# Mask copies by ScalarE into PSUM and a new written order for the first phase of a fused attention and feed-forward kernel

## The chip, the core and the metric

The kernel runs on one core of one Trainium2 chip. The core has a matrix engine (TensorE, in the profile PE, with its weight loads as PEld), VectorE (DVE), ScalarE (ACT), GpSimd (POOL), SyncE (SP, which only starts transfers here), and 16 DMA engines that all queues share. The engines work through their own instruction streams in order and wait for one another on semaphores. Matmul results land in PSUM, which has eight banks of 128x512 float32 here; everything else lies in SBUF.

The metric is device time in microseconds, the median of several runs. Less is better.

## The reference

Two computations follow each other. First a banded attention: 8 batches, 8 heads, 576 positions, head size 64, float32; a query sees itself and the 63 positions before it. Then a feed-forward layer on the 4608 rows of 512 that come out:

```python
scores = scale * np.matmul(q, k.transpose(0, 1, 3, 2))
mask = (rel >= 0) & (rel < window)            # rel = query - key, window = 64
scores = np.where(mask, scores, -1000000000.0)
scores = scores - np.max(scores, axis=-1, keepdims=True)
attn = np.exp(scores)
attn = attn / (np.sum(attn, axis=-1, keepdims=True) + 1e-09)
attn_out = np.matmul(attn, v)
...
h = x @ w_in                                  # 4608x512 @ 512x2048
g = np.maximum(0.01 * h, h)
out = g @ w_out                               # 4608x2048 @ 2048x512
```

`w_in` and `w_out` come as float64 and are turned into float32 on the chip.

## The kernel before, in words

**Attention.** The work is cut into 72 units, one unit being 64 queries of one batch against the 128 keys that its band can touch, all eight heads at once. Two units make a pair `m`; a pair's scores fill two tiles, one for the even and one for the odd heads, numbered `b = 2m` and `b = 2m + 1`. Scores lie with the keys on the partitions, so the maximum over keys goes across partitions, which GpSimd does.

**Feed-forward.** Each float32 factor is split into a high and a low part, and a product is three matmuls. The rows are taken in nine chunks of 512. The first three are computed plainly (`mm1` for the first layer, `mm2` for the second), a later part of the kernel does the others with fewer products. Weights are made ready in 32 pieces, each in seven steps: `raw` (transfer from HBM), `bits`, `sign` (VectorE), `abs` (ScalarE), `clamp`, `join` (VectorE), `chi` (high part, ScalarE, and for even pieces a transfer of the joined weights to HBM), `rest` (low part, VectorE). Both operands of all these VectorE steps lie in SBUF.

**The order.** Two things set what stands where in the instruction streams. The first phase, in which pairs 0 to 7 go through attention and most weights are made ready, is written out by hand as the string `ORDER` (line 54); each word is a step and a number, and each engine, and each DMA queue, gets its steps in the order of the words. What stands behind the `|` of that string and all later work is put in order by a small planner (`arrange`) with its own estimates of durations; the change leaves that part alone. The words:

- `q`, `k`, `v`: loads for a pair, on SP. `raw` 0 to 2 also on SP, later ones on ScalarE's queue.
- `S` scores of a pair on PE, with the masks before them (`scores`, `add_mask`; lines 278 and 312 in the profile); `Z` adds the mask of pair 0 behind its scores; `X` idle matmuls on a zeroed tile that keep PE busy (line 503).
- `E` (`shield`, lines 322 and 324) takes a score tile from PSUM to SBUF, by VectorE for the first two, by ScalarE later; `P` the maximum over partitions on GpSimd (line 332); up to `b = 3` the maximum is subtracted by a matmul into the score bank (`N`, line 346), later by VectorE (`sub`, line 337); `exp` on ScalarE.
- `V` product with the values and the sums of a row (line 367, 16 matmuls a tile); `sm`, `rec`, `y` sum, reciprocal and division on VectorE, from PSUM; `T` turns the result (line 393); `H` and `L` split it into high and low part (ScalarE, VectorE; lines 397 and 401).
- `M` and `W` first and second layer of one piece (lines 431 and 467), `lk`, `gh`, `gl` the leaky step and its split in between (ScalarE, ScalarE, VectorE). The first six jobs are half chunks. `ev` takes a finished bank out.

**Masks.** The mask of a pair is added to its scores in PSUM: a matmul of the identity (`unit`) with the mask (`away`) opens the bank, and the 64 small matmuls of the scores accumulate on it. The tile of the even heads is the bank with tag `s`, that of the odd heads `t`; pairs 1 and 3 use two output banks (`o0`, `o1`). `turn` puts pairs 0 and 1 into the bank `o3` and all others into `s`.

**Loads.** Of the transfers on SP and ScalarE's queue, eight can be under way at a time; a ninth is issued when an earlier one has landed. A load of a tile that is used again also waits for the last matmuls that read it.

Of the kernel before, what the change touches and what calls it, by code (L numbers as in the profile page):

```python
# [59 lines left out]
sm6 sign5 sm7 rest4 rec7 rec6 rest3 M2 E8 abs5 y7 y6 T3 bits6 sign6 W1 lk2 H3 L3 clamp5 P8 M3 gh2 gl2 join5 v4 k5 q5  # L60
E9 S5 v5 q6 k6 raw8 lk3 gh3 chi5 abs6 sub8 bits7 exp8 gl3 M4 lk4 rest5 sign7 clamp6 W2 V8 P9 abs7 sub9 join6 gh4 raw9
M5 bits8 gl4 E10 sm8 sign8 exp9 chi6 W3 P10 clamp7 rec8 y8 join7 rest6 lk5 abs8 clamp8 gh5 V9 M6 W4 gl5 join8 bits9
sub10 sm9 sign9 rec9 y9 raw10 E11 raw11 chi7 P11 chi8 lk6 exp10 T4 gh6 abs9 rest8 rest7 bits10 M7 V10 W5 gl6 sign10
clamp9 H4 abs10 sub11 join9 L4 bits11 sm10 rec10 clamp10 y10 join10 lk7 raw12 exp11 gh7 gl7 S6 V11 chi9 rest9 sign11
W6 chi10 raw13 abs11 E13 E12 P12 rest10 sm11 bits12 clamp11 join11 rec11 y11 chi11 raw14 sign12 abs12 bits13 sign13
clamp12 sub12 join12 M8 T5 v6 q7 v7 k7 W7 lk8 gh8 H5 exp12 abs13 chi12 raw15 gl8 P13 bits14 L5 V12 sign14 clamp13
rest11 sub13 sm12 join13 rest12 rec12 S7 y12 E14 raw16 abs14 exp13 clamp14 join14 bits15 P14 W8 V13 M9 sub14 sm13
sign15 chi14 E15 exp14 chi13 abs15 lk9 gh9 P15 rec13 y13 V14 T6 rest14 rest13 sub15 M10 sm14 clamp15 gl9 rec14 join15
y14 exp15 raw17 H6 chi15 V15 W9 bits16 sign16 L6 lk10 gh10 abs16 raw18 sm15 rec15 gl10 y15 T7 H7 rest15 W10 clamp16
bits17 join16 sign17 L7 abs17 clamp17 join17 bits18 raw19 chi16 ev0 chi17 ev1 raw20 rest16 sign18 abs18 rest17 M11  # L70
bits19 clamp18 M12 lk11 gh11 gl11 lk12 gh12 sign19 join18 M13 W11 M14 gl12 abs19 raw21 chi18 lk13 bits20 clamp19
join19 chi19 raw22 sign20 rest18 rest19 W12 M15 gh13 gl13 abs20 W13 bits21 clamp20 sign21 join20 bits22 abs21 lk14
sign22 clamp21 join21 raw23 chi20 M16 gh14 gl14 W14 rest20 raw24 abs22 clamp22 join22 chi21 raw25 bits23 rest21 sign23
bits24 lk15 chi22 gh15 gl15 sign24 abs23 abs24 clamp23 join23 bits25 chi23 raw26 lk16 M17 W15 clamp24 sign25 rest22
# [30 lines left out]
def band_attention_ffn(ctx: ExitStack, tc: tile.TileContext, qk, vW, vL, w_in, w_out, eye_mask, out, outT):  # L105
# [162 lines left out]
    def quarter_scores(m, ps, begun, more=False):  # L268

        q = q_of(m)  # L270
        for w in range(UNITS):
            k = key_blocks(UNITS * m + w)
            for p in range(NP):
                for i in range(2):
                    for j in range(2):
# [2 lines left out]
                        nc.tensor.matmul(  # L278
                            ps[j][t, c : c + QB], k[i][s, p], q[s, w, p],
                            start=not begun and (not more or (w, p) == (0, 0)),  # L280
                            stop=not begun and not more or (w, p) == (UNITS - 1, NP - 1),
                        )
# [1144 lines left out]
```

## Time and profile before

| | |
|---|---|
| median of 3 runs | 850.51 us (849.96 to 850.99) |
| profiled execution | 850.4 us |
| its span, first to last instruction | 848.6 us |
| PE busy | 841.8 us, 99% |
| VectorE busy | 620.1 us, 73% |
| ScalarE busy | 375.7 us, 44% |
| GpSimd busy | 383.3 us, 45% |
| HBM read, written | 172.52 MB, 53.06 MB |

Times in the profile are microseconds from the start of the span. A line number names a line of the kernel before; `s<-away,unit` means that tile `s` is written from `away` and `unit`. Busy times of PE are modelled at their ends, so successive matmuls overlap; start to start is the time that a step takes on PE. Idle time of an engine is put down to what ended it.

The first phase lies in the first 130 us; the matmuls of the second chunk begin at 87.69 us.

### The profile page before, as it was taken

The page shows a single profiled execution, that of the slowest core. Times are in us where ns is not written, and L with a number is a line of the kernel's source. Part 1 is how long each engine was busy: PE and PEld are TensorE (multiplying, and loading weights), DVE is VectorE, ACT ScalarE, POOL GpSimd, SP SyncE. Part 2 cuts the span into 40 slices and gives each one's busy share as a digit, 9 for nine tenths or more (in the row PEclk, how much of TensorE's full clock was granted, in tenths as well). Part 3 has the DMA queues.
Part 4 walks back from the last instruction along what each step waited for, and adds up shares of the span by engine and source line. Part 5 has one row for each costly group of instructions (what it writes and reads, how often), then busy time and mean ns, then how long its engine had stood idle before and what let it go on. Part 6 is the DMA issues. An engine that isn't in the chain of part 4 may idle for free.

```text
span 848.6 us, 16788 instructions
## 1 busy us (share of the span) xinstructions
PE 841.8 (99%) x6778; PEld 686.3 (81%) x6778; DVE 620.1 (73%) x883; ACT 375.7 (44%) x605; POOL 383.3 (45%) x218
## 2 busy tenths in 40 slices
PE   8999999999999999999999999999999999999998
PEld 5887888888878888888888888888888888888886
DVE  6999885748768779867649987585679955446863
ACT  4665654333433354454444433443354533324431
POOL 5422000878888715587587757857111111111110
PEclk9999999999999999999999999999999999999999
DMA  9875756798899869999999999999998986777682
GB/s 324 273 233 155 253 162 235 264 284 271 288 307 323 301 212 286 314 305 317 333 351 358 365 351 318 365 310 311 242 272 235 238 248 196 198 198 198 193 211 92
DMA packets 127757, 226.80 MB, mean 267 GB/s; under 512 B 15552, under 2 KB 46400, under 8 KB 127680
## 3 DMA queue, kind: packets, MB, share of 16 engines
q0 software_dynamic: 51552, 90.18, 38.4%
q10 hardware_dynamic: 35664, 77.31, 27.9%
q1 hardware_dynamic: 40464, 58.24, 21.1%
q8 instruction: 53, 0.87, 0.4%
q14 instruction: 24, 0.20, 0.1%
HBM read 172.52 MB, written 53.06 MB: 266 GB/s over the span
## 4 chain that ended last, share of the span: by engine, by line
PE 97%; DVE 2%; DMA 0%; ACT 0%; issue 0%; ACTq 0%
PE m L1118 27%; PE z L1181 18%; PE acc L929 11%; PE h L920 11%; PE y L1138 10%; PE h L431 5%; PE acc L467 5%; PE s L278 4%; PE o L740 4%; PE o L367 1%; DMA qk<-qk 0%; PE t L393 0%; DVE raw L225 0%; PE s L312 0%; DVE w L242 0%; DVE raw L229 0%
## 5 line engine op out<-in xcount | busy, mean ns | idle before, releaser
L1118 PE MATMUL m<-pfew,p 128*128 128x512 f32 x720 | 169.4, 391 | 0.0
L1118 PEld LDWEIGHTS m<-pfew,p 128*128 128x128 f32 x720 | 134.5, 188 | 28.3
L1102 POOL DMA_DIRECT2D p<-w_first x42 | 31.8, 757 | 113.4 <-PE m L1118 61.0
L929 PE MATMUL acc<-p,gs 128*128 128x512 f32 x324 | 80.6, 394 | 0.0
L1127 DVE TENSOR_TENSOR p<-m,pxa 128x512 f32<-128x512 f32 x60 | 41.3, 689 | 47.0 <-PE m L1118 46.0
L681 POOL PARTITION_ALL_REDUCE g<-late_f x20 | 36.8, 1875 | 78.7 <-DVE late_f L666 72.0
L684 POOL PARTITION_ALL_REDUCE late_o<-late_f x20 | 66.1, 3329 | 12.2 <-ACT late_f L692 7.0
L1118 PE MATMUL m<-pxb,p 128*128 128x512 f32 x288 | 70.9, 391 | 0.0
L1130 ACT ACTIVATE p<-p 128x512 f32<-128x512 f32 x60 | 37.9, 631 | 73.6 <-DVE p L1127 73.5
L929 PEld LDWEIGHTS acc<-p,gs 128*128 128x128 f32 x324 | 59.8, 188 | 12.8
L1127 DVE TENSOR_TENSOR pxa<-m,pxa 128x512 f32<-128x512 f32 x60 | 41.4, 690 | 35.4 <-PE m L1118 34.7
L684 POOL PARTITION_ALL_REDUCE late_o<-e x18 | 59.5, 3336 | 8.5 <-ACT e L692 3.6
L1118 PEld LDWEIGHTS m<-pxb,p 128*128 128x128 f32 x288 | 53.7, 188 | 11.3
L684 POOL PARTITION_ALL_REDUCE late_o<-late_e x18 | 59.3, 3322 | 5.5 <-ACT late_e L692 5.2
L1181 PE MATMUL z<-gs,p 128*128 128x512 f32 x240 | 57.6, 389 | 0.0
L920 PE MATMUL h<-pxa,p 128*128 128x512 f32 x228 | 54.9, 390 | 0.0
L1102 POOL DMA_DIRECT2D p<-w_second x28 | 22.7, 811 | 68.5 <-PE z L1181 31.0
L1181 PEld LDWEIGHTS z<-gs,p 128*128 128x128 f32 x240 | 45.0, 188 | 9.4
L1181 PE MATMUL z<-third,p 128*128 128x512 f32 x216 | 51.9, 389 | 0.0
L1181 PE MATMUL z<-pxa,p 128*128 128x512 f32 x216 | 51.9, 389 | 0.0
L920 PEld LDWEIGHTS h<-pxa,p 128*128 128x128 f32 x228 | 42.7, 188 | 9.0
L1102 POOL DMA_DIRECT2D p<-w_sums x16 | 12.0, 747 | 80.2 <-PE z L1181 55.8
(193 smaller groups left out, 1775.3 us busy)
## 6 DMA issues: line engine op xcount, KB each, us to landing
p<-w_first POOLq DMA_DIRECT2D x42, 1024.0 KB, 6.9
p<-w_second POOLq DMA_DIRECT2D x28, 1024.0 KB, 8.3
p<-w_sums POOLq DMA_DIRECT2D x16, 1024.0 KB, 5.7
qk<-qk ACTq DMA_DIRECT2D x26, 512.0 KB, 5.8
pspare<-w_second ACTq DMA_DIRECT2D x16, 512.0 KB, 7.2
w_sums<-pspare ACTq DMA_DIRECT2D x16, 512.0 KB, 7.7
raw<-w_out ACTq DMA_DIRECT2D x15, 512.0 KB, 3.9
raw<-w_in ACTq DMA_DIRECT2D x14, 512.0 KB, 3.9
```

What stands on the lines that cost most here:

```text
L431: nc.tensor.matmul(ps, a[:, k, :], b[:, k, part], start=n == 0, stop=n == len(terms) - 1)
L467: nc.tensor.matmul(acc[c, i], a[:, ts], b, start=begin and n == 0, stop=end and n == 2)
L681: nc.gpsimd.partition_all_reduce(most_of(j), e_of(m)[:, j], P, ReduceOp.max)
L684: nc.gpsimd.partition_all_reduce(sum_of(j), e_of(m)[:, j], P, ReduceOp.add)
L920: nc.tensor.matmul(ps, a[:, k, :], b[:, k], start=i == 0, stop=i == len(terms) - 1)
L929: nc.tensor.matmul(acc[c, i], a[:, i * P : (i + 1) * P], b, start=begin and k == 0, stop=n in ends and k == 2)
L1102: nc.gpsimd.dma_start(to, of, max_dma_last_dim=2048)
L1118: nc.tensor.matmul(tiles[b], w[:, 256 * i + 128 * kt : 256 * i + 128 * kt + 128], x_part(OF_X[k], j, kt), start=begin and c == 0, stop=c = ...
L1127: nc.vector.tensor_tensor(to(), tiles[b], x(), ALU.add)
L1130: nc.scalar.activation(to(), to() if b is None else tiles[b], AF.Prelu, alpha=0.01)
L1138: nc.tensor.matmul(tiles[i], a, b, start=f == 0 and k == 0, stop=f == FT - 1 and k == 2)
L1181: nc.tensor.matmul(tiles[b + i], a, x, start=begin and f == 0 and c == 0, stop=f == half - 1 and c == 2, skip_group_check=not begin,)
```

## The change

Three edits and a new string.

1. `seed` (new, word `A`): for pairs 4 to 7 ScalarE copies the mask, repeated over the heads, from SBUF into the PSUM bank, and the scores accumulate on that. For pairs 4 and 5 it does so for both tiles, for pairs 6 and 7 for the odd heads' alone; the even heads' mask stays a matmul there.
2. `turn` of pairs 2 and 3 goes to the bank `o3` too, instead of `s`.
3. `ORDER` is new up to the `|`. It has the same words and four more, `A4` to `A7`. In each engine's stream steps change places: the first idle matmuls are nine ahead of `S0` and none behind it; four others move ahead of `V2`; `S1` comes ahead of `Z0`; `T2` and `V6` stand between `M0` and `M1`; VectorE's steps on weights and on attention are interleaved in another way; and SP's loads begin `q0 raw0 q1 k1 raw1 k3 raw2 k2 v1 v0 q2 k4 q3 v2` where they began `q0 k1 raw0 q1 raw1 v0 q2 k2 raw2 v1 k3 q3 v2`.

```diff
+SEEDED, TURNED_OVER = 4, 6
...
 ORDER = """
-q0 X6 S0 k1 raw0 q1 E0 P0 E1 bits0 sign0 raw1 v0 q2 k2 P1 X3 Z0 Z1 S1 abs0 E2 N0 exp0 X1 N1 bits1 sign1 abs1 clamp0
-join0 clamp1 V0 sm0 join1 exp1 V1 E3 S2 chi0 raw2 chi1 raw3 rec0 sm1 rec1 bits2 sign2 y1 y0 P2 P3 N2 raw4 E4 rest1
-rest0 E5 exp2 N3 exp3 T0 v1 V2 V3 k3 q3 abs2 H0 S3 v2 v3 q4 k4 sm2 P4 sub4 P5 rec2 sm3 L0 y2 rec3 clamp2 y3 exp4 V4 E6
-T1 join2 H1 sub5 sm4 bits3 rec4 L1 exp5 X4 V5 P6 raw5 chi2 sign3 abs3 E7 bits4 rest2 sub6 sm5 clamp3 rec5 y4 y5 sign4
-P7 M0 lk0 exp6 gh0 M1 abs4 gl0 T2 W0 join3 sub7 bits5 clamp4 V6 lk1 H2 exp7 raw6 L2 gh1 join4 V7 S4 chi4 raw7 chi3 gl1
...
+q0 X3 X6 raw0 S0 q1 k1 E0 P0 bits0 E1 sign0 P1 raw1 S1 Z0 abs0 k3 bits1 sign1 Z1 clamp0 raw2 k2 v1 N0 v0 E2 bits2 abs1
+sign2 P2 N1 join0 X1 exp0 V0 clamp1 exp1 V1 sm0 q2 E3 chi0 rec0 abs2 join1 S2 chi1 raw3 P3 y0 E4 P4 sm1 rest0 k4 q3
+clamp2 rec1 N2 N3 y1 exp2 rest1 v2 X4 raw4 exp3 E5 V2 q4 join2 V3 v3 T0 sm2 rec2 H0 sub4 S3 sm3 y2 rec3 exp4 L0 y3 V4
+k5 P5 A4 bits3 sub5 bits4 sm4 T1 E6 rec4 y4 H1 S4 exp5 P6 raw5 sign3 L1 V5 sub6 E7 chi2 sign4 exp6 abs3 sm5 rec5 P7 y5
+M0 rest2 T2 lk0 abs4 V6 gh0 clamp3 join3 clamp4 sub7 raw6 join4 chi3 gl0 exp7 chi4 bits5 M1 sign5 V7 sm7 rec7 rest4 y7
+E8 P8 q6 W0 lk1 sm6 H2 raw7 gh1 rec6 L2 y6 gl1 rest3 E9 M2 bits6 T3 abs5 lk2 H3 gh2 sign6 L3 q5 clamp5 join5 abs6
+clamp6 W1 A5 v4 gl2 sub8 join6 chi5 P9 M3 raw8 bits7 S5 lk3 exp8 sign7 raw9 gh3 chi6 rest5 gl3 abs7 M4 lk4 sub9 V8 sm8
...
     def scores(m):
-        if m in (1, 3):
-            ps = [ps_o.tile([P, 512], F32, tag=f"o{j}", name=f"s{m}_{j}") for j in range(2)]
-        else:
-            ps = [bank(t, f"s{m}_{j}") for j, t in enumerate("st")]
-        for j in range(2):
-            probs[2 * m + j] = ps[j]
+        open_scores(m, range(2 if m < SEEDED else m >= TURNED_OVER))
         if m == 0:
-            quarter_scores(m, ps, False, True)
+            quarter_scores(m, [probs[j] for j in range(2)], False, True)
             return
-        for x in ps:
-            add_mask(m, x, True)
-        quarter_scores(m, ps, True)
+        for j in range(2 if m < SEEDED else m >= TURNED_OVER):
+            add_mask(m, probs[2 * m + j], True)
+        seeded = () if m < SEEDED else range(m >= TURNED_OVER, 2)
+        quarter_scores(m, [probs[2 * m + j] for j in range(2)], True, skip=seeded)
+
+    def open_scores(m, which):
+        for j in which:
+            pool, tag = (ps_o, f"o{j}") if m in (1, 3) else (ps_e, "st"[j])
+            probs[2 * m + j] = pool.tile([P, 512], F32, tag=tag, name=f"s{m}_{j}")
+
+    def seed(m):
+        open_scores(m, range(m >= TURNED_OVER, 2))
+        a = mask_of(UNITS * m).bitcast(F32)
+        n = a.shape[1]
+        a = flat(a)[:, None, :].broadcast_to([P, H // n, n * QB])
+        for j in range(m >= TURNED_OVER, 2):
+            nc.scalar.copy(probs[2 * m + j].rearrange("a (b c) -> a b c", c=n * QB), a)
...
     def turn(m):
         y = ys.pop(m)
-        pool, tag = (ps_o, "o3") if m < 2 else (ps_e, "s")
+        pool, tag = (ps_o, "o3") if m < 4 else (ps_e, "s")
```

More of the change, by code (lines that the diff above doesn't have):

```diff
@@ L60 @@
[L60 to L74, printed above, removed]
@@ new lines @@
+k5 P5 A4 bits3 sub5 bits4 sm4 T1 E6 rec4 y4 H1 S4 exp5 P6 raw5 sign3 L1 V5 sub6 E7 chi2 sign4 exp6 abs3 sm5 rec5 P7 y5
+M0 rest2 T2 lk0 abs4 V6 gh0 clamp3 join3 clamp4 sub7 raw6 join4 chi3 gl0 exp7 chi4 bits5 M1 sign5 V7 sm7 rec7 rest4 y7
+E8 P8 q6 W0 lk1 sm6 H2 raw7 gh1 rec6 L2 y6 gl1 rest3 E9 M2 bits6 T3 abs5 lk2 H3 gh2 sign6 L3 q5 clamp5 join5 abs6
+clamp6 W1 A5 v4 gl2 sub8 join6 chi5 P9 M3 raw8 bits7 S5 lk3 exp8 sign7 raw9 gh3 chi6 rest5 gl3 abs7 M4 lk4 sub9 V8 sm8
+clamp7 E10 rec8 rest6 W2 y8 join7 bits8 M5 P10 gh4 exp9 chi7 gl4 V9 sign8 W3 lk5 M6 raw10 sm9 bits9 abs8 v5 E11 rec9
@@ new lines @@
+sub10 clamp8 gh5 join8 gl5 sign9 rest7 chi8 W4 exp10 abs9 y9 raw11 lk6 gh6 A6 v6 clamp9 join9 P11 bits10 sign10 V10
+raw12 rest8 W5 sub11 T4 abs10 k6 clamp10 H4 M7 join10 chi9 L4 sm10 q7 raw13 rest9 rec10 bits11 chi10 gl6 y10 exp11 lk7
+gh7 sign11 S6 V11 bits12 sign12 rest10 W6 abs11 clamp11 sm11 abs12 E12 rec11 M8 join11 y11 gl7 T5 E13 clamp12 W7 raw14
+bits13 A7 chi11 lk8 rest11 H5 sign13 abs13 join12 P12 sub12 L5 raw15 clamp13 k7 exp12 V12 gh8 bits14 S7 v7 gl8 q8 P13
+W8 join13 sign14 chi12 sub13 rest12 sm12 raw16 E14 abs14 chi13 rec12 y12 exp13 V13 clamp14 join14 P14 bits15 sm13
@@ new lines @@
+sign15 sub14 M9 chi14 raw17 E15 exp14 rest14 rec13 y13 abs15 bits16 lk9 clamp15 V14 rest13 T6 gh9 H6 P15 sm14 join15
+raw18 rec14 sub15 exp15 y14 chi15 gl9 M10 sign16 V15 abs16 L6 lk10 W9 sm15 rest15 bits17 rec15 y15 gh10 clamp16 gl10
+join16 T7 H7 L7 sign17 bits18 W10 raw19 sign18 ev0 chi16 abs18 abs17 M11 clamp17 lk11 join17 M12 bits19 ev1 raw20 gh11
+rest16 clamp18 M13 join18 gl11 W11 raw21 sign19 lk12 chi17 abs19 clamp19 rest17 gh12 gl12 join19 chi18 M14 bits21
+raw22 bits20 chi19 W12 lk13 sign20 gh13 sign21 gl13 rest19 abs20 abs21 clamp21 lk14 clamp20 rest18 join20 bits22 raw23
@@ L78 @@
+M16 sign22 chi20 join21 chi21 gh14 M15 gl14 rest20 abs22 clamp22 join22 raw24 W13 rest21 raw25 bits23 sign23 W14 abs23
+lk15 gh15 chi22 clamp23 gl15 bits24 sign24 W15 join23 lk16 abs24 M17 bits25 sign25 raw26 chi23 gh16 abs25 rest22
+clamp24 join24 gl16 clamp25 raw27 chi24 M18 lk17 rest23 bits26 join25 sign26 gh17 gl17 raw28 bits27 chi25 W16 abs26
+rest24 W17 v8 sign27 rest25 abs27 clamp26 lk18 gh18 clamp27 join26 join27 chi26 bits28 gl18 sign28 q9 chi27 rest26 k8
 |
@@ L262, in x_of, with quarter_scores @@
         return [x[:, :, w * QB : (w + UNITS) * QB] for x in xs[c]]
-    def quarter_scores(m, ps, begun, more=False):
+    def quarter_scores(m, ps, begun, more=False, skip=()):
         q = q_of(m)
@@ L280, in quarter_scores @@
                             start=not begun and (not more or (w, p) == (0, 0)),
-                            stop=not begun and not more or (w, p) == (UNITS - 1, NP - 1),
+                            stop=not begun and not more or (w, p) == (UNITS - 1, NP - 1), skip_group_check=j in skip,
                         )
@@ L508, in band_attention_ffn @@
     acts = dict(
-        S=scores, E=shield, Z=lambda b: add_mask(0, banks[b], False), P=top, N=take, sub=minus, exp=exps, V=values_q, sm=total, rec=inverse, y=product, T=turn, H=high_x, L=low_x,
+        A=seed, S=scores, E=shield, Z=lambda b: add_mask(0, banks[b], False), P=top, N=take, sub=minus, exp=exps, V=values_q, sm=total, rec=inverse, y=product, T=turn, H=high_x, L=low_x,
         raw=fetch_w, bits=bits, sign=sign, abs=size, clamp=clamp, join=join, chi=split, rest=rest, q=load_q, k=load_k, v=load_v,
```

3 lines of the change are left out of this document (removed).

## The prediction

> **What bounds the kernel now.** The page comes first: its span, and the chain of waits followed back from the last instruction. Then come the list of what the matmul engine (PE) waited for over the whole run, and the busy time of the engines in two stretches, 20.00 to 87.69 and 87.69 to 130 us. The columns of these two rows are PE, weight loads, VectorE (DVE), ScalarE (ACT), GpSimd (POOL), clock, DMA share and GB/s.
>
> ```profile
> span 848.6 us, 16788 instructions
> ...
> PE 97%; DVE 2%; DMA 0%; ACT 0%; issue 0%; ACTq 0%
> ```
>
> ```profile
> PE idle L503 <- DVE p L514: 1.5, 1, 1.5
> ...
> PE o L367 <- DVE sm L379: 0.2, 1, 0.2
> ```
>
> ```profile
> 20.00:87.69 67.69, 66.67 (x781) 53.86 (x781) 65.47 (x148) 44.17 (x82) 22.29 (x11) 1.00 0.69 212
> 87.69:130.00 42.31, 42.31 (x188) 35.07 (x187) 34.79 (x65) 23.22 (x39) 0.00 (x0) 1.00 0.70 228
> ```
>
> PE carries 97% of the chain, and its five waits (first and last row above), 2.9 us together, all lie ahead of 27 us. After that it is never idle, so whatever the first phase gains or loses goes through to the end one for one. Up to 87.69 us VectorE is busy for 65.47 of 67.69 us, so it is nearly as tight as PE: 2.2 us idle. After 87.69 it has 7.5 us free in 42. The change is therefore worth what it does to the start of the matmuls at 87.69 (M11 of the order).
>
> Four views of the first 34 us decide that. First the PE timeline (start, duration, line, operands, number).
>
> ```profile
> 1.45 2.93 PE L503 MATMUL idle<-p 128*128 128x512 f32 x6 [1.45 <-DVE p L514]
> 4.74 1.98 PE L278 MATMUL s<-qk 64*64 64x64 f32 x64 [0.37 <-DMA qk<-qk]
> ...
> 12.63 1.44 PE L367 MATMUL o<-v,e 128*64 128x65 f32 x32
> ...
> 15.76 1.13 PE L346 MATMUL s<-p,p 128*128 128x512 f32 x2
> ...
> 17.61 0.66 PE L393 MATMUL t<-unit,y 128*128 128x128 f32 x4
> 18.20 1.15 PE L367 MATMUL o<-p,p 128*64 128x65 f32 x32
> 19.28 0.73 PE L312 MATMUL s<-away,unit 128*128 128x512 f32 x2
> ...
> 22.36 1.17 PE L503 MATMUL idle<-p 128*128 128x512 f32 x4
> ...
> 26.60 1.69 PE L431 MATMUL h<-pxa,pfew 128*128 128x256 f32 x12 [0.47 <-ACT g L436]
> 28.13 0.60 PE L393 MATMUL t<-unit,y 128*128 128x128 f32 x4
> 28.49 1.63 PE L467 MATMUL acc<-pfew,gs 128*128 128x512 f32 x6
> 30.05 1.33 PE L367 MATMUL o<-p,e 128*64 128x65 f32 x32
> 31.30 0.73 PE L312 MATMUL s<-away,unit 128*128 128x512 f32 x2
> 31.96 0.27 PE L278 MATMUL s<-qk,p 64*64 64x64 f32 x2
> ...
> 33.05 1.96 PE L431 MATMUL h<-pxa,pfew 128*128 128x256 f32 x12
> ```
>
> Start to start, a pair of masks is 0.66 us (31.30 to 31.96), scores are 1.09 (to 33.05), a pair of values products (32 matmuls, V2 V3) 1.08 (18.20 to 19.28), so one V 0.55 to 0.6, two maxima subtractions (N2 N3) 1.85 (15.76 to 17.61), half a first layer (M1) 1.53 (26.60 to 28.13), half a second layer (W0) 1.56 (28.49 to 30.05), a turning (T2) 0.36.
>
> **The change part by part.** *The masks.* Pairs 4 and 5 lose two mask matmuls each, pairs 6 and 7 one each. Pair 4's are 0.66 us (above). The rows of pairs 5 and 6, each with the first row of the scores behind it:
>
> ```profile
> 38.50 0.63 PE L312 MATMUL s<-away,unit 128*128 128x512 f32 x2
> 39.06 0.27 PE L278 MATMUL s<-qk,qk 64*64 64x64 f32 x2
> ...
> 57.03 0.62 PE L312 MATMUL s<-away,unit 128*128 128x512 f32 x2
> 57.58 0.27 PE L278 MATMUL s<-qk,qk 64*64 64x64 f32 x2
> ```
>
> Pair 5 gives 0.56, pair 6 half of 0.55; for pair 7 I take pair 6's half to pair 4's, 0.28 to 0.33. That is 0.56 + 0.28 + 0.3 = 1.15 us for the pairs behind 33 us, and with pair 4 1.8 us. In their place ScalarE makes six copies of 128x512 into PSUM. No such copy from SBUF is in the trace; the nearest row writes PSUM from PSUM:
>
> ```profile
> 131.41 0.58 ACT L934 ACTIVATE h<-h 128x512 f32<-128x512 f32 x1 [3.99 <-PE h L920]
> ```
>
> Six at 0.5 to 0.6 are 3.0 to 3.6 us on an engine that is busy 44.17 of 67.69 us. Three of the four groups wait on nothing late. The first (A4) stands ahead of the shields of pair 3 and holds these, and so GpSimd's sixth and seventh maximum, by up to 1.1 us; I take 0.3, because the scores the shields read are done at about the same time. It can gain nothing there.
>
> *The loads.* The order also rearranges the SP queue, and this is the part I hold to be dearest. Before, its first loads are q0 k1 raw0 q1 raw1 v0 q2 k2 raw2 v1 k3 q3; after, q0 raw0 q1 k1 raw1 k3 raw2 k2 v1 v0 q2 k4 q3. The values of pair 0 (v0) go from sixth to tenth. The rows are the issues of raw1, v0 and v1 on SP, each with the time from issue to landing  (asked for one by one), and the engines' busy time from 10 to 12 us:
>
> ```profile
> 2.59 0.61 SPq L210 DMA_DIRECT2D raw<-w_out  x1
> DMA to landing us min/median/max: 6.9/6.9/6.9
> 3.25 0.67 SPq L174 DMA_DIRECT2D v<-vW  x1
> DMA to landing us min/median/max: 7.6/7.6/7.6
> 6.51 0.56 SPq L174 DMA_DIRECT2D p<-vW  x1
> DMA to landing us min/median/max: 9.0/9.0/9.0
> 10.00:12.00 2.00, 1.88 (x16) 0.82 (x9) 1.97 (x3) 1.55 (x4) 2.00 (x2) 1.00 1.05 403
> ```
>
> So raw1 lands at 9.5, v0 at 10.9, v1 at 15.5, with the DMA engines full (share 1.05). They land in the order of issue and are paced by bytes. In the changed queue the same 2272 KB stand up to raw1, and between raw1 and the landing of v0 lie k3, raw2, k2, v1 and v0 itself, 2064 KB. That is exactly what lies between raw1 and v1 before (v0, q2, k2, raw2, v1), which took 6.0 us. By the pace of v0 alone (520 KB in 1.36 us) it would be 5.4. So v0 lands between 14.9 and 15.5; I take 15.1. The first product with values (V0), at 12.63 before, waits for it, and all of PE stands behind it.
>
> [...]
>
> *The other moves at the front.* Nine idle matmuls instead of six stand ahead of the first scores. At 2.93 us for six they end by 5.8 at the latest; with the last one's end overlapped I take 5.4, so these scores start 0.7 us later than 4.74, and so does the whole chain of maxima (N1 near 13.3). The late v0 covers this; without it, it costs 0.7.
>
> *From V0 on.* PE now has, in order: V0 V1 1.25, S2 with masks 1.75, N2 N3 1.85, four idles 1.1, V2 V3 1.1, T0 0.4, S3 1.75, V4 0.6, T1 0.4, S4 1.1 without masks, V5 0.6, M0 1.55, T2 0.35, V6 0.6, M1 1.55, V7 0.65, W0 1.5. The sum is 18.1 us, with no wait of M1 on the leaky step, because T2 and V6 stand between. 15.1 + 18.1 = 33.2. Before, the same work is done at 33.05. But GpSimd has to follow:
>
> ```profile
> 20.18 2.00 POOL L332 PARTITION_ALL_REDUCE g<-e  x1 [1.25 <-DVE sm L374]
> 23.22 1.88 POOL L332 PARTITION_ALL_REDUCE g<-e  x1 [1.03 <-DVE sm L374]
> ```
>
> One maximum follows the other in 3.0 us. S2 ends at 18.1, so the fifth starts near 18.7, the eighth near 27.7, and its subtraction and exponential end near 31.8; V7 would be due at 31.1. I put 1.2 us for this, the 0.3 of A4 and T2's wait for y5 together. That makes 34.4, or +1.35. Then the masks behind it give 1.15 back: +0.2. VectorE, whose step behind V2 (the sum, 19.27 before) moves to 21.4, enters the dense stretch 1.3 us late, about as late as PE itself; for the steps of it that PE then finds unfinished I add an estimate of 0.3. The sum is +0.5.
>
> *VectorE beside GpSimd.* Here is a maximum, a step of VectorE in SBUF that begins beside it, the same step alone, and the sum behind V2:
>
> ```profile
> 11.43 2.07 POOL L332 PARTITION_ALL_REDUCE p<-p  x1
> 11.50 1.33 DVE L237 TENSOR_SCALAR raw<-raw 128x512 f32<-128x512 f32 x1
> 13.48 0.42 DVE L237 TENSOR_SCALAR raw<-raw 128x512 f32<-128x512 f32 x1
> 19.27 0.15 DVE L374 TENSOR_SCALAR sm<-o 128x4 f32<-128x4 f32 x1
> ```
>
> A collision costs 0.9 us. In the new order VectorE still has only SBUF steps beside the first four maxima, so these stay, and wait for V0 anyway. Behind the fifth to the seventh maximum it now has PSUM steps (sm, y, L), worth up to 0.3 us each; as many SBUF steps (clamp, rest) stand beside later ones. I take nothing, with bounds of 2 us gain and 1 us loss.
>
> [...]
>
> **The rivals.** *Faster:* v0 is in time, because the loads aren't served in order or the queue is drained faster than I read. Then V0 starts at about 13.4 (the nine idles), 18.1 us of work end at 31.5, or 31.8 with the eighth maximum; that is -1.25, with the masks -2.4, and a few collisions less, -2.6: 847.9. For it speaks that PE's list is 2.5 us shorter; against it, that every landing of the first 17 us fits the bytes.
>
> *Slower:* VectorE becomes the bound from 20 to 88 us. It has 2.2 us idle there; the sum behind V2 comes 2.1 us later, and what stands behind it in VectorE's order (the weights' last steps, which PE waits for) with it. It decides as soon as VectorE's delay exceeds the slack of the weights' steps; then the masks' gain is lost, since PE waits anyway, and the end moves by those 2.1 and up to 0.5 of A4: 853.1. Against it speaks that PE itself is late there, and so asks later.
>
> *The masks alone count:* -1.8, 848.7, if early loss and early gain cancel. I count it to the faster case.
>
> **How the numbers follow.** The profiled execution is 850.4 us with a span of 848.6, the median of the runs 850.5. The forecast is 850.5 + 0.5 = 851.0. Its own range, with v0 between 14.9 and 15.5 and the waits of 1.2 between none and 2, is 849.3 to 852.5. I give it 0.42, the faster cases 0.33, the slower 0.25. About 0.2%, 1.7 us, can be told from no change. The range that holds 8 in 10 reaches to both rivals: 847.3 to 853.6. Faster 0.34, same 0.40, slower 0.26.
>
> **What would show it.** Right: in the changed trace the first L367 matmuls start at 14.9 to 15.5 and their releaser is the load of v; the first row of M2's matmuls is near 34.4; the L312 rows at 31, 38.5 are gone; M11 starts within 1 us of 87.69. Wrong: L367 starts before 14, or M11 starts below 86 (faster), or PE shows waits on L251 or L337 between 34 and 88 (slower).

## The result, and the profile after

The changed kernel takes 856.61 us (median of 5 runs, 856.36 to 858.18) where the kernel before takes 850.36 beside it (5 runs, 849.96 to 850.99): the ratio is 1.0077, with a 95% interval of 1.0065 to 1.0088. It is slower by 6.2 us. The forecast was 851.0, with a range of 849.3 to 852.5 of its own and of 847.3 to 853.6 for 8 in 10.

The profiled execution is the longest of the five (858.18). Line numbers from about 300 on are 9 higher than before: V is L376, N L355, M L440, W L476, `rest` L251, `sub` L346, the maxima L341. First the page: its span, and the chain of waits by engine.

```profile
span 856.4 us, 16779 instructions
...
PE 87%; DMA 5%; DVE 4%; POOL 1%; issue 1%; ACT 1%; SPq 0%; ACTq 0%; DVEq 0%; POOLq 0%
```

PE had 97% of that chain. Now 5% belong to transfers and 4% to VectorE. Most of the transfers' share is not the first phase, though: three transfers behind 350 us alone make up 28 us of the chain. In the first 95 us the chain has 10.5 us of transfers, 5.0 of them through the row with `qk` below, and nearly all of it from 35 to 48 us is VectorE. What PE waited for in the first phase stands in its list:

```profile
PE o L376 <- ACT raw L233: 2.6, 1, 2.6
...
PE s L355 <- POOL p L341: 0.8, 1, 0.8
PE h L440 <- DVE pfew L251: 0.8, 1, 0.8
PE o L376 <- DMA qk<-qk: 0.7, 1, 0.7
PE t L402 <- DVE y L395: 0.6, 2, 0.5
...
PE o L376 <- ACT e L362: 0.5, 1, 0.5
```

The first row is V0's wait. It is put down to ScalarE, but the load of v0 says otherwise: it is issued at 7.35 us and takes 8.3 (SP's queue, size and time to landing, from 7.3 to 7.4 us), so it lands at 15.65, and V0 starts at 15.82. The row with `qk` is V10, at 58.05, and I take it to be no load either: V10 starts 0.67 us after the start of VectorE's division y9 (57.38), and in five other runs with the new rest of the order this distance is the same, 0.66 to 0.67 us. In one of these the list itself names VectorE.

```profile
v<-vW SPq DMA_DIRECT2D x1, 520.0 KB, 8.3
```

PE's timeline of the changed kernel, with the first row of M2 at 37.49 and that of M11 at 94.03:

```profile
15.82 1.79 PE L376 MATMUL o<-v,e 128*64 128x65 f32 x32 [2.64 <-ACT raw L233]
...
29.93 1.57 PE L440 MATMUL h<-pxa,pfew 128*128 128x256 f32 x11 [0.25 <-DVE pxa L410]
31.97 0.63 PE L402 MATMUL t<-unit,y 128*128 128x128 f32 x4 [0.47 <-DVE y L395]
...
35.38 0.69 PE L376 MATMUL o<-p,e 128*64 128x65 f32 x16 [0.55 <-ACT e L362]
...
37.49 0.40 PE L440 MATMUL h<-pxa,pfew 128*128 128x256 f32 x2
38.66 1.45 PE L440 MATMUL h<-pxa,pfew 128*128 128x256 f32 x10 [0.78 <-DVE pfew L251]
...
94.03 0.61 PE L440 MATMUL h<-pxb,pfew 128*128 128x512 f32 x2
```

V0 is 3.2 us late (12.63 before), M2 4.4 (33.05), M11 6.3 (87.69). The 6.3 at M11 are the whole loss of 6.2; in this one execution another 1.4 us came behind 376 us, which the runs near 856.4, to go by their times, did not have.

Two things more are in the busy times by stretch (columns as in the prediction: length, PE, weight loads, VectorE, ScalarE, GpSimd, clock, DMA share, GB/s). The first three rows surround V0, the last goes from M2 to M11.

```profile
13.18:15.82 2.64, 0.00 (x1) 0.03 (x1) 2.52 (x4) 2.10 (x4) 2.37 (x2) 1.00 1.06 406
16.00:18.00 2.00, 2.00 (x33) 1.88 (x31) 1.18 (x5) 0.23 (x1) 0.40 (x1) 0.53 0.38 144
18.00:20.00 2.00, 2.00 (x66) 1.35 (x65) 1.97 (x7) 0.39 (x1) 0.00 (x0) 0.62 0.48 106
37.49:94.03 56.54, 54.39 (x542) 43.53 (x540) 55.73 (x115) 36.97 (x69) 16.37 (x8) 1.00 0.60 186
```

After the pause the granted clock is 0.53 and 0.62 for two stretches of 2 us. And from M2 to M11 VectorE is busy for 55.73 of 56.54 us. The same stretch of the kernel before:

```profile
33.05:87.69 54.64, 54.60 (x551) 43.87 (x545) 52.42 (x113) 35.63 (x66) 16.53 (x8) 1.00 0.65 196
```

There PE was full and VectorE had 2.2 us free. Now VectorE is full and PE has 2.1 us free, though four mask matmuls have gone from it. VectorE's steps of weights beside GpSimd's maxima are longer. Of many, here are one maximum (GpSimd's row) and three of VectorE's steps, the first beside it and the others beside the next two maxima (49.57 and 54.34). Alone such steps take 0.42 (L225) and 0.69 us (L242).

```profile
45.24 2.29 POOL L341 PARTITION_ALL_REDUCE g<-e  x1 [6.43 <-DVE e L346]
```

```profile
45.59 1.26 DVE L225 TENSOR_SCALAR raw<-raw 128x512 uint32<-128x512 uint32 x1
...
50.43 1.20 DVE L242 SCALAR_TENSOR_TENSOR w<-raw 128x512 uint32<-128x512 uint32 x1
54.48 1.44 DVE L242 SCALAR_TENSOR_TENSOR w<-raw 128x512 uint32<-128x512 uint32 x1
```

It is not that there are more of them. By the timelines of both engines 17 SBUF steps of 256 or 512 columns begin beside P8 to P15 before, and 17 after. But before, one of them is half a microsecond or more longer than alone, and after, eight are. What differs is the moment at which they begin. Before, steps that read PSUM (sum, division) or only four columns (reciprocal) mostly stand at the start of a maximum, and the SBUF step follows about 0.8 us or more behind the start. After, four SBUF steps begin 0.1 to 0.4 us behind it. One maximum of the kernel before, with what VectorE does beside it:

```profile
44.59 2.05 POOL L332 PARTITION_ALL_REDUCE g<-e  x1 [3.62 <-ACT e L324]
```

```profile
45.12 0.42 DVE L386 TENSOR_TENSOR y<-o,sm 128x256 f32<-128x256 f32 x1
45.46 0.98 DVE L242 SCALAR_TENSOR_TENSOR w<-raw 128x512 uint32<-128x512 uint32 x1
```

### The profile page after: what moved, and what is told of

It is laid out like the page before. It is cut to its first block, busy times and chain, and to the rows that moved or that the text cites. A ratio compares the mean times of both kernels' runs of the same rounds, so it can differ in the third digit from the quotient of the medians.

```text
span 856.4 us, 16779 instructions
## 1 busy us (share of the span) xinstructions
PE 843.0 (98%) x6772; PEld 686.5 (80%) x6772; DVE 621.6 (73%) x883; ACT 378.8 (44%) x611; POOL 383.0 (45%) x218
## 4 chain that ended last, share of the span: by engine, by line
PE 87%; DMA 5%; DVE 4%; POOL 1%; issue 1%; ACT 1%; SPq 0%; ACTq 0%; DVEq 0%; POOLq 0%
PE m L1127 24%; PE z L1190 18%; PE acc L938 11%; PE h L929 10%; PE y L1147 6%; PE acc L476 5%; PE h L440 4%; PE s L278 4%; PE o L749 3%; DMA pspare<-w_second 2%; PE o L376 1%; DMA late_r<-rows 1%; DMA rows<-late_c 1%; POOL late_o L693 1%; PE idle L512 1%
## 5 line engine op out<-in xcount | busy, mean ns | idle before, releaser
L1127 PEld LDWEIGHTS m<-pxb,p 128*128 128x128 f32 x288 | 53.6, 188 | 12.0 <-DVE pxa L1136 0.7
L341 POOL PARTITION_ALL_REDUCE g<-e x13 | 26.2, 2013 | 51.3 <-ACT e L333 12.5
```

The costliest lines, as they stand in the source:

```text
L1127: nc.tensor.matmul(tiles[b], w[:, 256 * i + 128 * kt : 256 * i + 128 * kt + 128], x_part(OF_X[k], j, kt), start=begin and c == 0, stop=c = ...
```

## The experiments

Each time is a median with its range and number of runs; "before" is 850.25 to 850.58 in all groups. The orders are shown by the words that move. In kernels with one more line of `ORDER`, line numbers are 10 higher than before.

### The loads: put back, and taken alone

The changed kernel with SP's first twelve loads in the old sequence, nothing else changed:

```diff
-q0 X3 X6 raw0 S0 q1 k1 ... raw1 ... k3 ... raw2 k2 v1 N0 v0 ... q2 ... k4 q3
+q0 k1 raw0 q1 raw1 v0 q2 k2 raw2 v1 k3 q3 X3 X6 S0 ... N0 ... k4
```

> The changed kernel with SP's first twelve loads in the order of the kernel before (q0 k1 raw0 q1 raw1 v0 q2 k2 raw2 v1 k3 q3); nothing else differs. Theory L (the late v0 is the loss: 2.6 us of wait, then some 3.4 us of matmuls at half clock, and VectorE idle behind it): V0 starts near 13.4, no row at half clock, and the time falls by 4 to 8 us from 856.6, to 848 to 852. Theory V (the new order of VectorE's steps makes VectorE the bound from 34 to 94 us, and the loads only hide it): at least 854.

Measured: 854.58 (853.99 to 856.45, 5 runs), ratio 1.0048 (1.0036 to 1.0061). V0 is back at 13.17 and the clock stays at 1.00, but only 2.0 of the 6.2 us come back: the time is in the range of theory V and not of theory L. VectorE's timeline shows one new wait, for the third weights, which the new order wants earlier than the old queue brings them:

```profile
13.52 0.50 DVE L226 TENSOR_SCALAR raw<-raw 128x512 uint32<-128x512 uint32 x1 [1.42 <-DMA raw<-w_in]
```

The converse, the old kernel with the new order of loads:

```diff
-q0 X6 S0 k1 raw0 q1 ... raw1 v0 q2 k2 ... raw2 ... v1 ... k3 q3
+q0 raw0 q1 k1 raw1 k3 raw2 k2 v1 v0 q2 X6 S0 ... S1 k4 q3
```

> The kernel before with only SP's first loads in the order of the changed kernel (q0 raw0 q1 k1 raw1 k3 raw2 k2 v1 v0 q2 k4 q3). Theory L: v0 lands near 15.6 and V0 waits 3 us, the clock halves once: 853.5 to 856. Theory V: the loads are covered, at most 851.5.

Measured: 855.51 (854.23 to 855.76, 5 runs), ratio 1.0055 (1.0042 to 1.0067). In its list of PE's waits and in its busy times by stretch:

```profile
PE o L367 <- DMA v<-vW: 3.3, 1, 3.3
```

```profile
16.00:18.00 2.00, 2.00 (x33) 1.88 (x33) 0.88 (x4) 0.11 (x1) 0.00 (x0) 0.50 0.41 157
18.00:20.00 2.00, 2.00 (x38) 1.35 (x42) 1.93 (x7) 0.51 (x1) 0.00 (x0) 0.50 0.55 137
20.00:22.00 2.00, 2.00 (x42) 1.37 (x35) 1.25 (x3) 0.89 (x2) 0.20 (x1) 0.50 1.00 391
```

The loads alone cost 5 us in the old order: 3.3 of waiting, and 6 us at half clock behind it. This is theory L's range. So the loads are worth 5 us in one order and 2 in the other: the parts do not add up. I take this to mean that in the new order something else is late as well.

### The clock

The changed kernel with 14 idle matmuls in front of V0 instead of one, so that PE has no pause:

```diff
-sign2 P2 N1 join0 X1 exp0 V0 clamp1
+sign2 P2 N1 join0 X14 exp0 V0 clamp1
```

> The changed kernel with fourteen idle matmuls in place of one ahead of V0, so that TensorE has no pause while it waits for v0. Theory L with the clock as part of the loss: no half clock, the products with values, masks and scores behind V0 take 1.2 us less, 855.4 or some less. If the clock costs nothing that counts: 856.6. If the idle matmuls reach past the landing: 857.

Measured: 856.00 (855.20 to 856.15, 5 runs), ratio 1.0061 (1.0047 to 1.0074). The stretch behind V0 again:

```profile
16.00:18.00 2.00, 1.89 (x35) 1.34 (x34) 0.98 (x4) 0.03 (x1) 0.41 (x1) 1.00 0.32 123
```

The clock is 1.00, M2 stands 3.41 late instead of 4.44, M11 5.47 instead of 6.34, and the median is 0.6 lower. The idle matmuls reach past the landing of v0, though: V0 starts at 16.26 here, 0.44 later than in the changed kernel. From V0 to M2 this run needs 20.2 us instead of 21.7. So the halved clock costs 1.0 us at M2 as the run stands, and some 1.5 if the late start is counted against it; at the end 0.6 to 0.9 are left.

### v0 in time, and raw2 too

The changed kernel with v0 sixth as before, and raw2 directly behind it:

```diff
-q0 X3 X6 raw0 S0 q1 k1 ... raw1 ... k3 ... raw2 k2 v1 N0 v0 ... q2 ... k4 q3
+q0 raw0 q1 k1 raw1 v0 raw2 q2 k2 v1 k3 q3 X3 X6 S0 ... N0 ... k4
```

> The changed kernel with v0 as the sixth load again, as before, and raw2 (whose bits come early in the new VectorE order) right behind it, the keys and queries behind that. Theory B (half of what the old load order left over is raw2 that came too late for the new order, 1.42 us of idle VectorE): V0 at 13.2 us, no idle time ahead of bits2, 852-853 in all. Theory C (the stretched steps from 30 us on carry the loss, and a VectorE that starts earlier only meets them earlier): V0 at 13.2, and 854-855, as with the loads put back whole.

Measured: 853.72 (852.83 to 854.40, 5 runs), ratio 1.0037 (1.0024 to 1.0049). V0 is at 13.10, bits2 waits for nothing, and 2.9 of the 6.2 us are back. The time lies between the two expectations. The other 3.3 us are neither v0 nor raw2; the runs that follow look for them. In this run's profile (852.83, its fastest execution, 2.4 us above the profile of before) M2 stands 1.0 us late and M11 2.4.

### The masks alone

The changed code (seeds and the other bank) with the old order and A4 to A7 put into it:

```diff
-... exp4 V4 ... E9 S5 ... E11 raw11 ... E13 E12 P12
+... exp4 A4 V4 ... E9 A5 S5 ... E11 A6 raw11 ... E13 E12 A7 P12
```

> The code of the changed kernel (ScalarE's mask copies, turnings of pairs 2 and 3 in bank o3) with the order of the kernel before; A4 stands behind exp4, A5 behind E9, A6 behind E11, A7 behind E12. If the six mask matmuls count in full: 1.8 us less than before, 848.6. If ScalarE's copies come late or hold up the shields: 850.4 or more.

Measured: 849.85 (849.41 to 851.51, 11 runs), ratio 0.9994 (0.9985 to 1.0002): the same. PE gets 1.68 us shorter at S4 to S7 (0.66, 0.56, 0.22, 0.24, start to start), but new waits stand on its timeline:

```profile
22.64 0.27 PE L279 MATMUL s<-p 64*64 64x64 f32 x1 [1.51 <-issue]
...
34.62 1.46 PE L441 MATMUL h<-pxa,pfew 128*128 128x256 f32 x10 [0.35 <-DVE pfew L252]
69.55 0.49 PE L322 MATMUL s<-away,unit 128*128 128x512 f32 x1 [0.32 <-DVE pxb L411]
74.44 0.69 PE L377 MATMUL o<-v,e 128*64 128x65 f32 x16 [0.34 <-DVE y L396]
```

The last three, 1.0 us, are waits for VectorE. (The first is no part of the masks; the last section comes back to it.)

Two attempts to keep the gain. One lets VectorE's bits0 begin ahead of the maximum P0. In the old order it begins 0.4 us behind the start of P0 (7.98, P0 at 7.57) and takes 0.90 us instead of 0.42:

```diff
-q0 X6 S0 k1 raw0 q1 E0 P0 E1 bits0 sign0 raw1 v0
+q0 raw0 k1 q1 raw1 v0 ... X6 S0 E0 bits0 P0 E1 sign0
```

> The old order with ScalarE's masks (849.85 us), and two edits at the front: raw0 ahead of k1 on SP, and bits0 right behind E0, so that VectorE's first step begins ahead of the maximum P0 and isn't stretched by it. Theory F (VectorE's stream from its first step sets M2, so that what starts earlier ends earlier): VectorE gains 0.5 us at bits0 and keeps it, 849.0-849.5. Theory G (v0, which lands 0.3 us later or at the same time, and TensorE's own 20 us set V0 and M2): 849.6-850.3, the same.

Measured: 850.19 (849.50 to 852.68, 11 runs), ratio 0.9998 (0.9989 to 1.0007). M11 is 0.23 us earlier than with the masks alone, too little to see in the time, which is theory G's.

The other moves the steps that the new waits name. In a first version I took rest3 for the one that M2 waits for:

```diff
-... chi4 raw7 chi3 gl1 sm6 sign5 sm7 rest4 ... gl8 P13 bits14 L5 ... join13 rest12 rec12 S7 y12
+... chi3 join4 V7 S4 chi4 gl1 sm6 rest3 sign5 sm7 rest4 ... L5 P13 bits14 gl8 ... rec12 S7 y12 join13 rest12
```

> The old order with ScalarE's masks (849.85 us), all maxima in place, and the steps that the three new waits name put a little earlier: chi3 ahead of chi4 and rest3 ahead of rest4 (M2), H5 ahead of the leak of step 8 and L5 ahead of bits14 and gl8 (S7), y12 ahead of join13 and rest12 (V13). Theory R (the gain is lost only where VectorE comes last at these three places): 848.7-849.3, faster than before. If the lost time moves on to the next step of VectorE instead, 849.6-850.2.

Measured: 849.77 (849.20 to 852.88, 12 runs), ratio 0.9994 (0.9984 to 1.0004). The two late waits are smaller, but M2 now waits 0.98 for rest4, which I had pushed back. The second version has rest4 early instead:

```diff
-... sub7 bits5 clamp4 ... gl1 sm6 sign5 sm7 rest4 ... gl8 P13 bits14 L5 ... join13 rest12 rec12 S7 y12
+... sub7 clamp4 ... gl1 sm6 rest4 bits5 sign5 sm7 ... L5 P13 bits14 gl8 ... rec12 S7 y12 join13 rest12
```

> The old order with ScalarE's masks (849.85 us), with the steps that its new waits name put earlier: rest4, for which M2 waits, ahead of sign5 and bits5, H5 and L5 ahead of the leak and the low half of step 8, y12 ahead of join13 and rest12. If the masks' gain is lost only where VectorE comes last at these three places, M2's wait of 0.35 and the two of 0.4 us go, 848.7-849.3, faster than before. If VectorE as a whole sets the pace, the waits move on, 849.5-850.

Measured: 851.49 (851.19 to 853.00, 11 runs), ratio 1.0017 (1.0008 to 1.0026). M2's wait is gone, and two larger ones are there in its place, at T3 and V13:

```profile
35.68 0.63 PE L403 MATMUL t<-unit,y 128*128 128x128 f32 x4 [1.82 <-DVE y L396]
74.31 0.69 PE L377 MATMUL o<-v,e 128*64 128x65 f32 x16 [1.06 <-ACT e L363]
```

Neither came out as hoped for (848.7 to 849.3). In both, moving VectorE's steps moved the wait and did not shorten it. So I have no version with all its maxima that is faster than the kernel before by more than can be measured.

### VectorE beside GpSimd: the maxima P8 to P15 left out

Three kernels leave these maxima out, so the scores of pairs 4 to 7 are taken less the maximum of tile 7; the steps of all other engines stay.

```diff
-        nc.gpsimd.partition_all_reduce(mx, probs[b], P, ReduceOp.max)
+        if b < 8:
+            nc.gpsimd.partition_all_reduce(mx, probs[b], P, ReduceOp.max)
```

In the new order with the old loads:

> The first loads in the old order and the rest in the new one (854.58 us with all maxima), and GpSimd's maxima P8 to P15 left out: the scores of pairs 4 to 7 are taken less the maximum of tile 7, and the work of the other engines stays the same. Theory C (the new order puts more of VectorE's SBUF steps beside these maxima, and they stretch: 5.5 us of stretching between 30 and 90 us where the old order has 2.4): the time falls by 3 to 5 us, to 849.5-851.5, and stands no more than 1.5 us above the old order without these maxima. Theory Q (the new order of the steps itself keeps TensorE waiting, whatever GpSimd does): it falls no more than the old order does, and stands 3.5 to 4.5 us above it.

In the kernel before:

> The kernel before, with the maxima P8 to P15 left out in the same way (the scores of pairs 4 to 7 are taken less the maximum of tile 7). Its VectorE is stretched by 2.4 us between 30 and 90 us and waits for little else there. Theory C: 848.0-849.0, a gain of 1.5 to 2.4 us, half of what the new order gains. Theory Q: it gains what the new order gains, whatever that is (0 to 2 us), and the distance between the two stays near 4.

In the old order with the masks:

> The old order with ScalarE's masks (849.85 us), and the maxima P8 to P15 left out (the scores of pairs 4 to 7 are taken less the maximum of tile 7). The masks take 1.68 us from TensorE at S4 to S7, but 1.2 us come back as waits for VectorE at M2, S7 and W8. Theory R (VectorE, stretched beside GpSimd, re-spends the gain): without the maxima the waits go and the whole gain stands, 848.6-849.2, while the old order without these maxima gained nothing (850.28). Theory T (something else takes it back): 849.6-850.1.

Measured: 853.12 (852.36 to 854.11, 5 runs) where it was 854.58; 850.28 (849.96 to 851.14, 11 runs) where it was 850.5; 849.46 (848.83 to 852.96, 12 runs) where it was 849.85. The stretch from M2 to M11 shows more than the medians. New order with all maxima (the loads put back), then without:

```profile
35.21:91.28 56.07, 54.43 (x542) 43.54 (x540) 55.27 (x115) 36.49 (x67) 15.88 (x8) 1.00 0.60 189
```

```profile
36.28:90.18 53.90, 53.63 (x542) 43.43 (x540) 50.08 (x115) 36.39 (x67) 0.00 (x0) 1.00 0.62 198
```

The old order without them (with them: 54.64 long, VectorE 52.42), and the masks in the old order with and without:

```profile
32.69:87.33 54.64, 54.60 (x550) 43.86 (x546) 50.25 (x113) 35.64 (x66) 0.00 (x0) 1.00 0.60 196
```

```profile
33.77:88.63 54.86, 53.80 (x546) 43.32 (x542) 53.60 (x115) 37.92 (x70) 16.59 (x8) 1.00 0.60 196
```

```profile
32.28:86.48 54.20, 53.64 (x540) 43.33 (x541) 50.72 (x115) 37.90 (x70) 0.00 (x0) 1.00 0.62 199
```

VectorE's own work is 50.1 to 50.7 us in all three. GpSimd stretches it by 2.2 us in the old order (52.42 less 50.25) and by 5.2 in the new one (55.27 less 50.08). In the old order these 2.2 cost nothing, since PE's 54.6 are longer; the length is the same to 0.01 us. With the masks off PE its work falls to 53.6 to 53.8, VectorE's 53.6 reach it, and the gain is spent on waits. In the new order VectorE's 55.3 stand above PE's 53.6 and set the length: without the maxima the stretch is 2.2 us shorter. The time falls by 1.5, not by the 3 to 5 of the expectation: behind M2 the contention accounts for the loss, in front of M2 it does not.

None of the three times is quite what a theory had. The new order stands 2.8 us above the old one without these maxima, where theory C had at most 1.5 and theory Q 3.5 to 4.5. The old order gains 0.2, not theory C's 1.5 to 2.4. And 849.46 with the masks lies between theory R (up to 849.2) and theory T (from 849.6), in ranges that overlap. That VectorE spends the masks' gain is what the lengths show (54.86 and 54.20); the times alone don't.

### The front: TensorE's list, VectorE's list, a store

Up to M2 the kernel with v0 sixth waits for VectorE and ScalarE at M0, T2 and V7. Either engine's list was changed alone.

```diff
-N2 N3 y1 exp2 rest1 v2 X4 ... T1 E6 rec4 y4 H1 S4 ... M0 rest2 T2 lk0 abs4 V6 gh0 ... M1 sign5 V7
+N2 N3 y1 exp2 rest1 v2 ... T1 X4 E6 rec4 y4 H1 ... M0 rest2 lk0 abs4 V6 gh0 M1 T2 ... sign5 V7 S4
```

> The changed kernel with v0 sixth (853.72 us; M2 at 34.06 where before has 33.05) and TensorE's own steps between 18 and 34 us put back near the old places, all other engines' lists unchanged: the filler X4 behind T1, the scores S4 behind V7, M1 ahead of T2. Theory P (the new order of TensorE's steps uses its filler before it is needed, and so M0, T2 and M1 wait 1.9 us for L1, y5 and sub7): the waits at M0, T2 and M1 shrink by 1 us or more, M2 at 33.1 or earlier, 852.3-852.9. Theory D (VectorE itself is late with L1, y5 and sub7): the same work ends at the same moments, M2 within 0.4 us of 34.06, 853.3-854.

```diff
-rec4 y4 H1 S4 exp5 P6 raw5 sign3 L1 ... sign4 exp6 abs3 sm5 rec5 P7 y5 ... clamp3 join3 clamp4 sub7 ... exp7
+rec4 H1 L1 y4 S4 exp5 P6 raw5 sign3 ... exp6 sm5 rec5 P7 y5 sign4 abs3 ... clamp3 sub7 exp7 join3 clamp4
```

> The changed kernel with v0 sixth (853.72 us), TensorE's list unchanged, and three of VectorE's steps for the attention put ahead of steps on the weights: L1 behind rec4 (was behind bits3, bits4 and sign3), y5 ahead of sign4, sub7 (and exp7 on ScalarE) ahead of join3 and clamp4. Theory D (these three keep TensorE at M0, T2 and V7): M0's wait of 0.72 goes, T2's and V7's shrink, M2 at 33.0-33.4, and 852.4-853.0. Theory P (what counts is TensorE's order): M2 within 0.4 of 34.06, 853.3-854.

Measured: 854.08 (852.79 to 856.56, 6 runs) and 854.04 (852.96 to 855.33, 6 runs), both as before the edit (853.72). The profile of the first is its slowest execution, so only its time is read. In the second the waits at M0 and V7 became shorter, as expected of theory D, but M2 then waits for `rest` instead, and its second half starts later than with v0 sixth alone (35.46 against 34.75; the two rows, in this order). V0 itself starts 0.64 us later in this execution (13.74), so from V0 on nothing is gained and nothing lost:

```profile
35.46 1.45 PE L441 MATMUL h<-pxa,pfew 128*128 128x256 f32 x10 [0.91 <-DVE pfew L252]
```

```profile
34.75 1.45 PE L441 MATMUL h<-pxa,pfew 128*128 128x256 f32 x10 [0.28 <-DVE pfew L252]
```

Then the order was divided at M2: all engines take one order up to M2, and from the other order what is left.

```diff
-... rec6 rest3 M2 E8 abs5 y7 y6 T3 bits6 sign6 W1 lk2        (old, then old)
+... rec6 rest3 M2 k5 y7 E8 P8 q6 y6 E9 bits6 T3 abs5 lk2     (old, then new)
-... gl1 rest3 E9 M2 bits6 T3 abs5 lk2 H3 gh2 sign6 L3        (new, then new)
+... gl1 rest3 E9 M2 abs5 T3 bits6 sign6 W1 lk2 H3 L3         (new, then old)
```

> ScalarE's masks; every engine takes the old order up to M2, and the new order for all that is left behind it. With v0 sixth the new order as a whole costs 3.3 us. Theory D (VectorE's list at the front, 2.5 us longer up to the weights of step 4, carries it): M2 at 32.5-33.8, and no more than 0.5 us lost behind it, 849.5-850.5. Theory C (the steps beside the maxima P8 to P15 behind M2 carry at least as much): M11 1.0 us or more later against M2 than in the old order, 851-852.

> The other half: ScalarE's masks, v0 sixth, every engine takes the new order up to M2 and the old order for all that is left. Theory D: M2 near 34.06 and its lateness kept, 852.5-853.5. Theory C: 851-852, and this run's loss and the one of the old front with the new rest add up to 3.3 us.

Measured: 850.97 (850.49 to 852.49, 11 runs), ratio 1.0011 (1.0002 to 1.0020); and 853.43 (852.89 to 854.29, 5 runs), ratio 1.0036 (1.0024 to 1.0049). Against the masks in the old order (849.85) the new front costs 3.6 and the new rest 1.1. They add up to 4.7, more than the 3.9 of both together, so the division is only good to a us: by it two thirds to three quarters lie in front. By the profiles M2 stands at 32.33 with the old front and at 36.27 with the new one, but the second is the slowest execution of its kernel (854.29). In it VectorE waits at join2 for a store:

```profile
21.89 0.69 DVE L243 SCALAR_TENSOR_TENSOR w<-raw 128x512 uint32<-128x512 uint32 x1 [1.99 <-DMA w_single<-w]
```

join2 writes the buffer from which ScalarE's queue stores the first joined weights to HBM. In the old order it comes at 21.76 and does not wait; in the new one it comes 2 us earlier. PE then waits for V4, stands still from 22.07 to 24.16, and loses clock as behind the late v0 (columns as above):

```profile
24.16 0.69 PE L377 MATMUL o<-v,e 128*64 128x65 f32 x16 [2.08 <-ACT e L363]
```

```profile
24.00:26.00 2.00, 1.71 (x28) 1.27 (x32) 2.00 (x4) 1.75 (x5) 1.39 (x1) 0.81 0.26 93
26.00:28.00 2.00, 2.00 (x70) 1.88 (x68) 1.86 (x7) 1.00 (x2) 1.57 (x1) 0.50 0.34 57
28.00:30.00 2.00, 2.00 (x26) 1.91 (x23) 1.97 (x6) 1.09 (x3) 0.65 (x2) 0.84 0.78 268
```

In the changed kernel itself join2 starts at 20.14 and does not wait, since everything ahead of it waits for v0; so this wait is no part of the 6.2 us, only of the versions with v0 in time. One run moves join2 back:

```diff
-E5 V2 q4 join2 V3 v3 T0 sm2 rec2 H0 sub4 S3 sm3 y2 rec3 exp4 L0 y3
+E5 V2 q4 V3 v3 T0 sm2 rec2 H0 sub4 S3 sm3 y2 rec3 exp4 L0 join2 y3
```

> The changed kernel with v0 sixth (853.72 us), and VectorE's join2 behind L0 instead of ahead of the sum behind V2. join2 writes the buffer from which ScalarE's queue stores the first joined weights; in the new order it comes at 19.7-19.9 (old order 21.76), and in three profiles it waited 0.26, 1.28 and 1.99 us for that store to land, with the sum, the exponential of tile 4 and V4 behind it. Theory W (this wait is a part of the 3.3 us, and the one that differs between executions): no VectorE wait on the store, 852.4-853.2, in a narrower range than 852.83 to 854.4. Theory D alone (VectorE is late anyway, the wait only takes the place of others): 853.3-854.

Measured: 853.03 (852.56 to 854.55, 7 runs), ratio 1.0031 (1.0020 to 1.0043). That is 0.7 us less, with no wait for the store in its profile, as theory W has it; but the ranges overlap, this one is no narrower, and against an execution in which join2 waited only 0.26 us M2 did not move (34.26 against 34.06). By the medians the wait is 0.7 of the 3.3 us, but the runs don't show that firmly. In this profile M2 stands 1.9 us later than with the old front (32.33), and the stretch from M2 to M11 (56.03 us) is 1.2 us longer than with the masks in the old order (54.86): together they are about the 3.2 us between the medians (853.03 and 849.85).

What is left of the front, some 2 us, was not taken apart. VectorE is busy for 28.6 of the 30 us from 7 to 37 here, but so it is before (29.6), and the two lists show that no single one of the moved steps is to blame. Two things stand in the record that no run moved. In the profiles of these two kernels V0 starts at 13.10 and 13.45 instead of 12.63, about what the prediction had named for nine idle matmuls without the late v0 (0.7 us). And the new order has the divisions y6 and y7 (0.42 us each) ahead of the `rest` that M2 waits for: 60 steps of VectorE instead of 58.

## Why the prediction was wrong

The frame held: PE is the end, and what the front loses goes through. The sum of the terms did not: M11 was to be at 88.2 (87.69 + 0.5), and is at 94.03. The 5.8 us between divide like this. Three small slips matter little: V0 and V1 take 1.38 us in the kernel before (12.63 to 14.01), not 1.25; PE's list there is 20.4 us from V0 to M2, so the new one is 2.3 shorter, not 2.5; and the bounds named for v0 and the waits give 849.6 to 852.2, not 849.3 to 852.5.

**The loads (0.7 us).** The mechanism was right, and the time nearly: v0 was to land between 14.9 and 15.5 (15.1 in the sum), and landed at 15.65. V0 stands at 15.82 instead of 15.1. From the landing of raw1 (9.2 in the changed kernel, 9.5 before) the same 2064 KB took 6.5 us, where they took 6.0 before: the order of issue and the bytes gave the landing to half a microsecond.

**The clock (1.0 us, or 1.5 with the late start of that run counted).** This step was not in the working at all. My own sum has V0 ready at 13.4 and starting at 15.1, and I did not ask what such a pause does to PE; it became 2.6 us.

**From V0 on (1.4 us, or 0.9).** I gave V0 to M2 18.1 us of work and 1.2 of waits; it took 21.7 with 1.0 to 1.5 of clock in it. The waits were looked for at the right places (T2 for y5, V7 behind the eighth maximum), M0's wait for L1 was missed. Start to start, M0 with the waits takes 2.68 us (29.29 to 31.97) for the 1.55 of the sum, and M1 with V7's wait 2.24 (33.14 to 35.38) for 1.55: this alone is 1.8 us of waits. "For the steps of it that PE then finds unfinished I add an estimate of 0.3" is the only term for a late VectorE, and it was far too small. VectorE had to wait for V0 and V2 itself (VectorE's timeline of the changed kernel),

```profile
16.78 0.16 DVE L383 TENSOR_SCALAR sm<-o 128x4 f32<-128x4 f32 x1 [1.05 <-PE o L376]
...
23.71 0.16 DVE L383 TENSOR_SCALAR sm<-o 128x4 f32<-128x4 f32 x1 [2.88 <-PE o L376]
```

and these 3.9 us of idle time came out of an engine that before had 2.2 to spare from 20 us to M11.

**Behind M2 (2.7 us).** "I take nothing, with bounds of 2 us gain and 1 us loss" for VectorE beside GpSimd is the single term that failed most. It counted collisions by number, and the number stayed the same (17). The price of one did not: more steps now begin right behind the start of a maximum, and VectorE is stretched by 5.2 us against 2.2 (the new order with the old loads, and the old order). These are 3.0 us more of VectorE's time; without the maxima the stretch from M2 to M11 is 2.2 us shorter, over twice my bound. I had compared the steps behind the fifth to seventh maximum one by one and let the later ones count as even. With it fell the masks' term: -1.15 behind M2 holds only while PE is the longer engine. The stretch from M2 to M11 became 1.9 us longer instead of 0.85 shorter. How much of this the front's late VectorE adds is not separated: behind the old front the new rest has 55.76 us from M2 to M11 (before 54.64, changed kernel 56.54), and costs 1.1 us in the time.

**The masks.** Sizes right: 1.68 us on PE instead of 1.8, and a copy of ScalarE is 0.59 us (the group of the six in the changed kernel), against 0.5 to 0.6 estimated.

```profile
L314 ACT COPY s<-away 128x512 f32<-128x512 f32 x6 | 3.4, 586 | 0.5 <-DVE y L395 0.5
```

The rival that the masks alone count (848.7) is out: alone they give 849.85.

**The nine idle matmuls** cost 1.2 us at S0 (5.97 against 4.74), not 0.7, and were covered by v0 as assumed.

**The rival that came true** is the slower one, VectorE as the bound, and its sign was there as named: a wait on L251 between 34 and 88 us, at 38.66. I gave it 0.25 and 853.1. Its mechanism was there, and its price of 2.6 us less than half of the 6.2: it counted VectorE's lateness at V2 once, and neither the stretching behind M2 nor the clock.

A single collision was a delay, as the prediction had it. Beside the maximum that starts at 45.24 and lasts 2.29 us, the step of 45.59 takes 1.26 us where it takes 0.42 alone, and ends at 46.85, 0.7 ahead of the maximum, so it did not wait for GpSimd's instruction to end, as far as GpSimd's spans, which are rough in the profile, can tell. Likewise in the kernel before, the step of 11.50 ends at 12.83, 0.7 ahead of the maximum beside it (11.43 and 2.07). But "a collision costs 0.9 us" is not one price: beside P8 to P15 it is 0 to 0.84 us, by when the step begins.
